# Windowed attention and a gated feed-forward on one core: regrouping the sums and products of an attention block, loading keys earlier, and halving the last projection

## Chip, cores, metric

One of the eight cores of a Trainium2 chip runs the whole kernel. The metric is device time in microseconds (us); lower is better. The profile's span is some 1.8 us shorter than the device time (335.7 and 337.54 for the profiled run of the kernel before). Executions of one kernel differ by some tenths of a us.

## The reference

Attention with a causal window of 64 positions over 8 batches, 8 heads, 576 positions and 64 values a head, then a gated feed-forward over the 4608 resulting rows of 512:

```python
scores = scale * np.matmul(q, k.transpose(0, 1, 3, 2))
mask = (rel >= 0) & (rel < 64)                  # rel = query position - key position
attn = softmax(np.where(mask, scores, -1e9))
x = np.matmul(attn, v)                          # (4608, 512) after the heads are joined
out = (silu(x @ w_gate) * (x @ w_val)) @ w_out  # 512 -> 1536 -> 512
```

## The kernel before

The rows are worked off in nine blocks `t` of 512. A block has an attention part, 12 pairs of gate matmuls (`gate_value`), and four projections (`project`). The projections of block `t - 1` run between the attention pieces of block `t`. One attention piece handles a pair `u` of heads:

- `scores`: 36 small matmuls on 64x64 tiles, an exponential on the scalar engine, and a mask product on the vector engine;
- `sums`: two matmuls with a weight of ones on 128x64 tiles, then a logarithm and the exponential of its negative on the scalar engine, which gives one over the sum;
- `values`: 16 matmuls on 128x64 tiles and a scaling on the vector engine.

The parts concerned (cuts marked by "..."):

```python
def values(t, u, o_ps):
    E = weights.pop((t, u))
    ...
    for m in range(8):
        for h in range(2):
            nc.tensor.matmul(blocks(o_ps[64 * h:64 * h + 64], t, m, m + 1), ..., blocks(E[:, h, :], t, m, m + 1))
    nc.vector.tensor_mul(xT[t][:, u, :], o_ps[:], inverse.pop((t, u)))

def products(t, u):
    sums(t, u, ...)
    values(t, u, ...)

# block 0's gates: block 1's keys are loaded at m = 3..6, cast at 7..10,
# transposed on the tensor engine at 8..11; queries are transposed from m = 10 on
...
# first phase: block 1's attention beside block 0's projections
for u in range(4):
    scores(1, u)
    if u % 2:
        project_part(0, (0, 1), halves, range(3 * u - 3, 3 * u + 3))
...
# every later phase
for u in range(8):
    if u < 4:
        scores(t, u)
    else:
        products(t, u - 4)
    if u % 2:
        project(t - 1, u // 2)
```

The softmax here doesn't subtract the row's maximum and nothing guards it: scores larger than these inputs give would overflow.

## Time and profile before

| | before |
|---|---|
| device time, median of the first 3 runs | 337.47 us |
| span of the profiled run | 335.7 us |
| tensor engine busy | 323.2 us, 96% |
| gate matmuls of block 1 begin at | 56.29 us |
| from one block's first gate to the next block's | 34.80 us |
| from the last block's first gate to the end of the span | 35.72 us |

The last three rows cut the run into start, seven equal periods and tail: 56.29 + 243.69 + 35.72. The starts are read from the tensor engine's timeline. A period is 20.7 us of gates and a phase of about 14 us of attention and projections. The first mark, as the timeline has it (start, length, what it was):

```profile
56.29 1.03 PE L306 MATMUL g_ps<-xT,wg 128*128 128x512 bf16 x4
```

One more row of the page of before, the busy share of the 16 DMA engines in 40 slices of 8.4 us (9 means 90% or more):

```profile
DMA  7999999999899499639931999199401320010013
```

After the first slice, the DMA engines are busy for 80% or more of the time until 100 us.

### The profile page before, as it was taken

The numbers are of one execution on the slowest core, as the hardware profiler recorded it, in microseconds if no ns is written. First come the engines' busy times: TensorE is split into PE (matmuls) and PEld (weight loads), VectorE is DVE, ScalarE is ACT, GpSimd is POOL, SyncE is SP. The second block draws the span as 40 slices with busy tenths as digits, with TensorE's granted clock in tenths as the row PEclk, the third lists the DMA queues.
The fourth block names the chain that finished last, engine by engine and source line by source line (L and its number), as shares of the span: only waits on it lengthen the run. The fifth ranks groups of instructions, "written<-read, shape, count | busy, mean of one in ns | idle before, by whom it ended". The sixth has DMA issues, their size and how long they took to land.

```text
span 335.7 us, 6932 instructions
## 1 busy us (share of the span) xinstructions
PE 323.2 (96%) x2683; PEld 153.9 (46%) x2729; DVE 214.2 (64%) x318; ACT 169.2 (50%) x241; POOL 137.8 (41%) x247
## 2 busy tenths in 40 slices
PE   8899799999999999999999999999999999999994
PEld 3444344444544454445444544444444444544441
DVE  5754766588667756785678656865786476753431
ACT  4764656336733763366435553565347633763300
POOL 5944345946767965256123896163200000000000
PEclk9999999999999999999999999999999999999999
DMA  7999999999899499639931999199401320010013
GB/s 261 205 202 226 229 188 223 125 205 215 147 248 186 52 176 234 124 58 209 185 89 20 170 180 167 12 189 177 111 0 48 79 56 3 23 72 31 3 32 94
DMA packets 83057, 44.12 MB, mean 131 GB/s; under 512 B 63824, under 2 KB 77648, under 8 KB 83024
## 3 DMA queue, kind: packets, MB, share of 16 engines
q0 software_dynamic: 49328, 22.56, 54.2%
q1 hardware_dynamic: 31680, 19.02, 20.6%
q10 hardware_dynamic: 2016, 2.10, 2.2%
q8 instruction: 21, 0.34, 0.4%
q14 instruction: 12, 0.10, 0.1%
HBM read 54.00 MB, written 9.44 MB: 189 GB/s over the span
## 4 chain that ended last, share of the span: by engine, by line
PE 88%; DMA 6%; DVE 3%; issue 2%; ACT 1%; DVEq 0%
PE g_ps L306 26%; PE v_ps L306 26%; PE o_ps L315 25%; PE s_ps L227 3%; DMA k_f<-in_k_dram 3%; PE ao_ps L271 3%; PE d_ps L245 3%; DMA q_f<-in_q_dram 1%; PE tp L174 1%; PE g_ps L286 1%; ACT E L233 1%; DVE kT L177 1%; PE v_ps L286 1%; DMA out_dram<-os__4409 1%; DMA out_dram<-os__4428 1%
## 5 line engine op out<-in xcount | busy, mean ns | idle before, releaser
L299 ACT ACTIVATE sg<-g_ps 128x512 f32<-128x512 f32 x108 | 64.4, 597 | 112.1 <-PE g_ps L306 79.9
L300 DVE TENSOR_TENSOR hT<-sg,v_ps 128x512 bf16<-128x512 f32 x108 | 74.9, 694 | 62.9 <-PE v_ps L306 59.9
L306 PE MATMUL v_ps<-xT,wv 128*128 128x512 bf16 x417 | 108.3, 379 | 0.5
L306 PE MATMUL g_ps<-xT,wg 128*128 128x512 bf16 x413 | 107.6, 379 | 0.5
L315 PE MATMUL o_ps<-wo,hT 128*128 128x512 bf16 x405 | 96.5, 380 | 1.6 <-issue 0.6
L107 POOL DMA_DIRECT2D k_s<-in_k_dram x112 | 60.7, 551 | 29.8 <-DMA q_s<-in_q_dram 20.5
L306 PEld LDWEIGHTS <-wv 128*128 128x128 bf16 x424 | 41.5, 98 | 50.0
L306 PEld LDWEIGHTS <-wg 128*128 128x128 bf16 x424 | 41.4, 98 | 49.5 <-issue 0.3
L315 PEld LDWEIGHTS <-hT 128*128 128x128 bf16 x432 | 39.6, 98 | 45.1 <-issue 0.4
L233 ACT ACTIVATE E<-s_ps 128x1024 bf16<-128x1024 f32 x36 | 35.2, 1021 | 8.4 <-PE s_ps L227 8.2
L277 DVE TENSOR_TENSOR xT<-ao_ps,r 128x512 bf16<-128x512 f32 x36 | 24.7, 691 | 22.7 <-ACT r L256 20.5
L196 DVE STREAM_TRANSPOSE kT<-k_s 128x512 bf16<-128x512 bf16 x28 | 35.9, 1284 | 0.0
L253 ACT ACTIVATE r<-d_ps 128x512 f32<-128x512 f32 (+1 forms) x35 | 21.0, 601 | 22.4 <-PE d_ps L245 22.4
L235 DVE TENSOR_TENSOR E<-E,mask 128x1024 bf16<-128x1024 bf16 x28 | 20.5, 739 | 11.5 <-ACT E L233 11.5
L87 POOL DMA_DIRECT2D q_s<-in_q_dram x28 | 15.3, 558 | 26.7 <-DVE qT L186 16.0
L148 POOL CAST v<-v_f 128x512 bf16<-128x512 f32 x22 | 14.3, 665 | 21.5 <-DMA v_f<-in_v_dram 17.5
L256 ACT ACTIVATE r<-r 128x512 f32<-128x512 f32 (+1 forms) x35 | 22.3, 641 | 1.1
L186 DVE STREAM_TRANSPOSE qT<-q_s 128x512 bf16<-128x512 bf16 x32 | 22.3, 702 | 0.0
L271 PEld LDWEIGHTS <-v 128*64 128x64 bf16 x576 | 13.8, 112 | 5.7 <-issue 1.7
L271 PE MATMUL ao_ps<-E,v 128*64 128x64 bf16 x576 | 15.3, 196 | 0.6 <-DVE v L156 0.6
L245 PE MATMUL d_ps<-E,ones 128*64 128x512 bf16 x72 | 13.9, 392 | 0.3
L227 PE MATMUL s_ps<-qT,kT 64*64 64x128 bf16 (+1 forms) x640 | 12.5, 211 | 0.2 <-DVE kT L177 0.2
(95 smaller groups left out, 175.6 us busy)
## 6 DMA issues: line engine op xcount, KB each, us to landing
q_s<-in_q_dram POOLq DMA_DIRECT2D x28, 248.0 KB, 6.7
k_s<-in_k_dram POOLq DMA_DIRECT2D x112, 56.0 KB, 5.2
v_f<-in_v_dram SPq DMA_DIRECT2D x22, 256.0 KB
v<-in_v_dram POOLq DMA_DIRECT2D x18, 128.0 KB, 4.8
k_f<-in_k_dram ACTq DMA_DIRECT2D x6, 256.0 KB
wo<-in_moe_w_out_dram POOLq DMA_DIRECT2D x3, 512.0 KB, 16.0
v<-v SPq DMA_DIRECT2D x6, 256.0 KB
v<-v SPq DMA_DIRECT2D x6, 192.0 KB
```

Of the source, the lines that this page charges most:

```text
L107: nc.gpsimd.dma_start(k_s[p0:p0 + 32, g, :, 0:w], k[b, a:H:2, s:s + P].rearrange("u (r e) d -> r u (e d)", e=4) [:, :, 32 * c:32 * c + w],)
L186: nc.vector.transpose(queries[t][:, u, :].rearrange("r (e x) -> r e x", e=16), staged[t][0][:, u].rearrange("r (e d) -> r e d", d=D)[:, :, ...
L196: nc.vector.transpose(dst[:, u, :].rearrange("r (g x e) -> r g e x", g=4, e=4), k_s[:, :, u].rearrange("r g (e d) -> r g e d", d=D)[:, :, ...
L227: nc.tensor.matmul(blocks(s_ps[64 * c:64 * c + 64, h], t, lo, hi), zero[r] if src is None else src[r, u, x:x + 64], blocks(qT[r], t, lo, h ...
L233: nc.scalar.activation(E[:], s_ps[:], AF.Exp, scale=0.125)
L245: nc.tensor.matmul(d_ps[64 * h:64 * h + 64], ones[:, 0:D], weights[t, u][:, h, :])
L271: nc.tensor.matmul(blocks(o_ps[64 * h:64 * h + 64], t, m, m + 1), (v1, v2)[m // 4][t % 2][:, m % 4, 2 * u + h, :] if t == LAST else (v2, v ...
L277: nc.vector.tensor_mul(xT[t][:, u, :], o_ps[:], inverse.pop((t, u)))
L299: nc.scalar.activation(sg[:], g_ps[:], AF.Silu)
L300: nc.vector.tensor_mul(hT[t][:, m, :], sg[:], v_ps[:])
L306: nc.tensor.matmul(ps[:], w[:, c, P * m:P * m + P], xT[t][:, c, :], start=(c == 0), stop=(c == 3),)
L315: nc.tensor.matmul(o_ps[:], hT[t][:, c, P * s:P * s + P], wo[:, c, :], start=(c == 0), stop=(c == 11),)
```

## The change

Its intent is to visit the small matmul tiles less often: in each phase the sums of pairs 0 and 1 follow the last scores, and the sums of pairs 2 and 3 and all four products form one group ahead of the last projection. With it come the edits of a sibling kernel (another version of the same program): keys of block 1 two gates earlier, another order at the start, a finer warm-up, and a last projection in two halves. The core of the diff, shortened and partly put in words:

```diff
-    def products(t, u):                      # sums and product of one pair
+    def finish_values(t):
+        for u in (2, 3):
+            sums(t, u, d_tile())
+        tiles = wide("ao_ps"), wide("ao_ps")
+        for u in range(4):
+            mix(t, u, tiles[u // 2][:, u % 2])      # the 16 matmuls
+        for u in range(4):
+            scale(t, u, tiles[u // 2][:, u % 2])    # the vector engine's product
...
+    def project_last(t, s):                  # two halves of 256 columns, own copies and stores
...
-    nc.vector.memset(ones[:], 1.0)
+    nc.vector.memset(ones[:, 0:P], 1.0)
+    nc.vector.memset(ones[:, P:512], 1.0)
-    keep_warm(7)
+    six warm-up matmuls of 128 columns, then keep_warm(6)
...
-    values(0, 0), values(0, 1), log_of(2), gates of m = 0, log_of(3), gates of m = 1
+    log_of(2), values(0, 0), values(0, 1), log_of(3), gates of m = 0 and 1
...
-        if 3 <= m < 7:      # key loads of block 1
+        if 1 <= m < 5:      # and casts, transposes two gates earlier, queries one
...
-            for u in range(8): (as above)
+            for u in range(4):
+                scores(t, u)
+                if u == 1:
+                    project(t - 1, 0)
+            for u in range(2):
+                sums(t, u, d_tile())
+            for s in (1, 2):
+                project(t - 1, s)
+            finish_values(t)
+            project(t - 1, 3)
...
-    for s in range(4):
+    for s in range(3):
         project(NT - 1, s)
+    project_last(NT - 1, 3)
```

The first phase gets the new grouping as well.

More of the change, by code (lines that the diff above doesn't have):

```diff
@@ L263, in sums, with mix @@
         inverse[t, u] = r
-    def values(t, u, o_ps):
+    def mix(t, u, o_ps):
         E = weights.pop((t, u))
-        if u == 0:
-            xT[t] = att.tile([P, 4, 512], BF16, name="xT", tag="xT")
         for m in range(8):
@@ L276, in values, with scale, wide, d_tile @@
                 )
-        nc.vector.tensor_mul(xT[t][:, u, :], o_ps[:], inverse.pop((t, u)))
-    def products(t, u):
-        sums(t, u, ps_f.tile([P, 512], FP32, name="d_ps", tag="v")[:])
-        values(t, u, ps_a.tile([P, 2, 512], FP32, name="ao_ps", tag="a")[:, 0])
+    def scale(t, u, o_ps):
+        if u == 0:
+            xT[t] = att.tile([P, 4, 512], BF16, name="xT", tag="xT")
+        nc.vector.tensor_mul(xT[t][:, u, :], o_ps, inverse.pop((t, u)))
+    def values(t, u, o_ps):
+        mix(t, u, o_ps)
+        scale(t, u, o_ps)
+    def wide(name):
+        return ps_a.tile([P, 2, 512], FP32, name=name, tag="a")
+    def d_tile():
+        return ps_f.tile([P, 512], FP32, name="d_ps", tag="v")[:]
+    def finish_values(t):
[6 more added lines that the diff above has]
+            scale(t, u, tiles[u // 2][:, u % 2])
     def gate_part(t, ms, tiles, c):
@@ L342, in project @@
         project_end(t, s, o_ps)
+    def project_last(t, s):
+        rows = out[S * batch(t):S * batch(t) + 512].rearrange("(r e) f -> e r f", e=16)
+        os_ = fsb.tile([P, 512], FP32, name="os_", tag="os_", bufs=3)
+        tiles = out_tile(), out_tile()
+        for x in range(2):
+            f = slice(256 * x, 256 * x + 256)
+            for c in range(12):
+                nc.tensor.matmul(
+                    tiles[x][:, 0:256], hT[t][:, c, P * s:P * s + P], wo[:, c, f],
+                    start=(c == 0), stop=(c == 11),
+                )
+            nc.vector.tensor_copy(os_[:, f], tiles[x][:, 0:256])
+            for i in range(4):
+                eng = nc.scalar if i % 2 else nc.sync
+                eng.dma_start(rows[4 * s + i][:, f], os_[32 * i:32 * i + 32, f])
     def set_exp():
@@ L368, in keep_warm @@
             nc.tensor.matmul(warm[0:D], ones[:, 0:D], ones[:])
-    keep_warm(7)
+    for _ in range(6):
+        nc.tensor.matmul(warm[0:D, 0:P], ones[:, 0:D], ones[:, 0:P])
+    keep_warm(6)
     nc.gpsimd.memset(tri[:], 1.0)
@@ L402, in shift_dma @@
         nc.sync.dma_start(dst, src)
-    def wide(name):
-        return ps_a.tile([P, 2, 512], FP32, name=name, tag="a")
     def join(copy, dst, src):
@@ L469, in log_of @@
         log(inverse[0, u], d_ps)
-    keep_warm(6)
+    keep_warm(5)
+    log_of(2)
     for u in range(2):
         values(0, u, ps_f.tile([P, 512], FP32, name="ao_ps", tag="gv"[u])[:])
-    log_of(2)
+    log_of(3)
     pairs = [gate_tiles() for _ in range(2)]
-    gate_part(0, (0,), pairs, 0)
-    log_of(3)
-    gate_part(0, (1,), pairs[1:], 0)
+    gate_part(0, (0, 1), pairs, 0)
     for u in (2, 3):
@@ L499 @@
             nc.vector.tensor_copy(mask[:, 1], mask[:, 0])
-        if 3 <= m < 7:
-            hs = slice(2 * m - 6, 2 * m - 4)
+        if 1 <= m < 5:
+            hs = slice(2 * m - 2, 2 * m)
             load_runs(nc.scalar, raw_k[:, hs], k, 1, hs)
-        if 7 <= m < 11:
-            u = m - 7
+        if 5 <= m < 9:
+            u = m - 5
             join(on_a, keys[:, u], raw_k[:, 2 * u:2 * u + 2])
-        if m >= 8:
-            u = m - 8
+        if 6 <= m < 10:
+            u = m - 6
             tp = ps_a.tile([P, 512], BF16, name="tp", tag="a")
@@ L510 @@
             split_k(kT[1][:, u, :], tp[:])
-        if m >= 10:
-            turn_q(1, m - 10)
-    turn_q(1, 2)
+        if m >= 9:
+            turn_q(1, m - 9)
     turn_q(1, 3)
@@ L527 @@
         shift_v(1, on_v, i, i + 1)
-    def d_tile():
-        return ps_f.tile([P, 512], FP32, name="d_ps", tag="v")[:]
     for u in range(2):
@@ L534 @@
     project(0, 2)
-    o_ps = out_tile()
-    for u in range(4):
-        if u < 2:
-            sums(1, u + 2, d_tile())
-        values(1, u, one("ao_ps"))
-        if u:
-            project_part(0, (3,), (o_ps,), range(4 * u - 4, 4 * u))
-    project_end(0, 3, o_ps)
+    finish_values(1)
+    project(0, 3)
     for t in range(1, NT):
@@ L546 @@
             set_exp()
-            for u in range(8):
-                if u < 4:
-                    scores(t, u)
-                else:
-                    products(t, u - 4)
-                if u % 2:
-                    project(t - 1, u // 2)
+            for u in range(4):
[8 more added lines that the diff above has]
+            project(t - 1, 3)
         set_silu()
```

## The prediction

> **What bounds the kernel now.** I read the page first (busy shares, then the chain that ended last), then the tensor engine's timeline piece by piece, then the timelines of the engines that issue loads.
>
> ```profile
> span 335.7 us, 6932 instructions
> PE 323.2 (96%) x2683; PEld 153.9 (46%) x2729; DVE 214.2 (64%) x318; ACT 169.2 (50%) x241; POOL 137.8 (41%) x247
> PE 88%; DMA 6%; DVE 3%; issue 2%; ACT 1%; DVEq 0%
> ```
>
> The tensor engine carries 88% of the chain. The clock row of the page is full in all 40 slices, so its matmuls cannot get cheaper; only the places where it waits or changes shape are to be had. In the timeline four 512-column matmuls start 0.86 us apart (160.69, 161.55, 162.41), 0.216 us each. The gate stage of 864 and the projection of 432 of them are 1296 x 0.216 = 280 us of the 335.7. The other 56 us are the start, eight attention phases and the tail.
>
> A steady phase is one attention block beside the four projections of the block before. Its two-pair stretch, from the tensor engine's timeline (start, length):
>
> ```profile
> 152.53 0.81 PE L315 MATMUL o_ps<-wo,hT 128*128 128x512 bf16 x3
> 153.27 0.41 PE L245 MATMUL d_ps<-E,ones 128*64 128x512 bf16 x2
> 153.51 0.42 PE L271 MATMUL ao_ps<-E,v 128*64 128x64 bf16 x16
> 153.76 0.39 PE L245 MATMUL d_ps<-E,ones 128*64 128x512 bf16 x2
> 153.98 0.42 PE L271 MATMUL ao_ps<-E,v 128*64 128x64 bf16 x16
> 154.33 0.82 PE L315 MATMUL o_ps<-wo,hT 128*128 128x512 bf16 x2
> ```
>
> No line shows an idle time: the engine never waits there for another. By starts the phase runs 146.70, 147.29, 149.99, 150.58, 153.27, 154.33, 157.03, 158.09, 160.69: scores 0.59, projection 2.70, scores 0.59, projection 2.69, two pairs 1.06, projection 2.70, two pairs 1.06, projection 2.60; 13.99 us. A projection of 12 x 0.216 is 2.59, so 0.10 of each 2.70 is the step to a smaller tile; the last, followed by gates of its own shape, lacks it.
>
> The one real wait is where the first phase begins (block 1 beside projections of block 0):
>
> ```profile
> 39.58 0.40 PE L174 MATMUL tp<-identb,k_b 128*128 128x128 bf16 x4
> 39.94 0.41 PE L227 MATMUL s_ps<-qT,kT 64*64 64x128 bf16 x16
> 42.02 0.22 PE L227 MATMUL s_ps<-qT,zero 64*64 64x64 bf16 x2 [1.66 <-DVE qT L186]
> 42.38 2.76 PE L315 MATMUL o_ps<-wo,hT 128*128 128x512 bf16 x11
> ```
>
> The second scores wait 1.66 us for a query transpose on the vector engine, which queued behind the last key copies; those waited for the late key load (the chain has a 9.63 us piece of that load from 29.26).
>
> **What the Trainium skill says.** "TensorEngine Tiling (Array Packing)", Key Properties: changing the tiling mode drains the engine. The trace agrees: 0.10 us in front of each smaller shape, and another 0.10 behind (ao products take 0.25 when products follow, 0.35 when a projection does). "DMA: Bandwidth & Descriptors", Queues, rings and completion order: each DMA engine goes round-robin between its queues. The page's DMA row is at nine tenths until some 100 us, and queue 0 alone took over a full share of the first 60 us, so an earlier key load displaces other loads and adds no bandwidth. "TensorE: Matmul & The Clock Gate", Part 1: the clock opens by a free-running window of about 3.4 us. The trace's warm-up matmuls are 0.427 apart from 1.53 us (cold) and 0.216 at 13 us; whether it opens earlier after the change no view can tell me.
>
> **The change part by part.**
>
> *Seven steady phases.* Before: four visits to small tiles. After: three, but the second goes scores, then sums (64x64 to 128x64), which is a mode change too. At the start scores take as long before 128x64 warm-up matmuls (12.39 to 12.73) as before 128x128 transposes (10.54 to 10.88), so that inner step costs what a way out costs. And two pairs of sums ahead of a projection leave late:
>
> ```profile
> 48.36 0.62 PE L245 MATMUL d_ps<-E,ones 128*64 128x512 bf16 x4
> 48.99 2.75 PE L315 MATMUL o_ps<-wo,hT 128*128 128x512 bf16 x12
> ```
>
> 0.63 for four sums, of which 2 x 0.216 is streaming. New phase: scores 0.59, projection 2.70, scores 0.59, sums 0.63, two projections 2.59 + 2.70, sums 0.24 + 0.22, products 3 x 0.25 + 0.35, projection 2.60: 13.96 against 13.99. So 7 x 0.03 = 0.2 us, almost nothing. New waits? The first sums need the masked weights of pair 0 and 1; masks of 0.69 start at 148.91 and 149.83, so are done at 150.52, while the sums would start at about 150.6: it just fits. The inversions and four scalings (0.69 each) end under the last projection.
>
> *First phase.* The four key loads go out two gates (3.45 us) earlier, the key transposes and the query transposes with them. The 1.66 wait goes, and scores take 0.59 in place of 2.44 (39.94 to 42.38). Two interleaved product visits also go. In block 0, the fourth sums no longer split the first gate matmuls:
>
> ```profile
> 16.38 0.38 PE L286 MATMUL v_ps<-xT,wv 128*128 128x512 bf16 x1
> 16.69 0.41 PE L245 MATMUL d_ps<-E,ones 128*64 128x512 bf16 x2
> 17.02 0.39 PE L286 MATMUL g_ps<-xT,wg 128*128 128x512 bf16 x1
> ```
>
> 16.16 to 17.56 becomes 4 x 0.216 + 0.10 = 0.96, a gain of 0.44. But the projections then meet their own weights. From the pool engine's timeline (brackets: what it waited for):
>
> ```profile
> 39.98 0.55 POOL L87 DMA_DIRECT2D q_s<-in_q_dram  x1 [2.15 <-DMA wo<-in_moe_w_out_dram]
> 42.55 0.54 POOL L87 DMA_DIRECT2D q_s<-in_q_dram  x1 [2.03 <-DMA wo<-in_moe_w_out_dram]
> ```
>
> The output weights come in thirds issued at 23.65, 26.53 and 27.84 and land 15.7 to 16.9 us later: at about 39.7, 42.3 and 44.8. Moving the key load inside a saturated stretch that ends after it leaves these times where they are. Without waits, projections would begin at about 39.6 and ask for the second third 8 matmuls later, at 41.3. It lands at 42.3, so I place that matmul at 42.37. Four matmuls (0.86), step and scores (0.10 + 0.59): 43.92. Four more: 44.78, where the last third has just landed (44.85); eight: 46.58. Step and sums 0.73: 47.31. Projection 2.59: 49.90. Step, sums, products 0.10 + 0.46 + 1.10: 51.56. Projection 2.59: 54.15. The gates began at 56.29, so 2.1 us are gained, including what the 0.44 can still give. The values of block 1 (last issue 35.06, median 13.8 us to landing) are there by about 48.9 and shifted by about 50.0, so products at 50.5 should not wait for them.
>
> *End.* The last projection goes in two halves of 256 columns. Today:
>
> ```profile
> 331.26 0.69 DVE L322 COPY os__4447<-o_ps 128x512 f32<-128x512 f32 x1 [1.90 <-DMA out_dram<-os__4428]
> 331.98 0.78 SPq L334 DMA_DIRECT2D out_dram<-os__4447  x2
> ```
>
> The skill ("Perfetto Trace Analysis", Optimizing Scalar/DVE Operations) gives the vector engine about 125 ns of overhead on PSUM. The trace has no 256-wide copy of this kind; as an estimate, (0.69 - 0.125)/2 + 0.125 = 0.41, so 0.28 less, minus 0.03 for 24 matmuls at 0.108 with one more start. The stores after it (some 3.7 us to the end of the span) keep most of their length at half the bytes. Gain 0.25.
>
> *Warm-up.* Memset and matmuls start perhaps 0.3 us earlier, but the transposes at 4.79 wait for the query load (3.27 us) and its cast (0.63): nothing, and an earlier clock would be swallowed by the weights at 42.3.
>
> Sum: 2.1 + 0.2 + 0.25 = 2.55; I keep 2.4, as a late key cast can delay gates by some tenths. 337.47 - 2.4 = 335.1.
>
> **Rivals.** (a) The small-tile visits cost more than starts show, and one fewer in seven phases gives 0.2 each: 1.4 us, about 333.9. Against it: the sums of projections, scores, sums and products above close to 0.03. (b) Sums right behind the last scores wait for the mask of pair 1, or four grouped products hold the score buffers and xT comes late: 0.3 x 7, about 337. Against it: the mask is done 0.1 before, and the scaling has 0.4 us and four gate matmuls to spare. (c) The earlier key load pushes gate weights or block 1's queries (issued 17.42 to 21.10, landing 13 to 15 us later, until 36.5) so late that the vector engine blocks: 1 us lost, 336.1. (d) The output weights land earlier or the wait is smaller: the first phase gains 3.2, about 334.
>
> **Range and chances.** (b) and (c) set the top, (a) and (d) the bottom: 333.7 to 336.4. Faster by 2% means below 330.7, which would need three times the sum: 2%. Slower by 2% needs a wait of over 1 us in each of seven phases: 1%.
>
> **What would show it.** Right: no 1.66 wait; an idle of about 1 us before an o_ps matmul at about 42.3 put down to output weights; gates of block 1 beginning near 54.2; steady phases of 13.9 to 14.0 us without idle; a last copy of about 0.4 us. Wrong: steady phases under 13.8 or over 14.2; idle before d_ps released by a mask; gates of block 0 delayed by weights.

## The result

334.94 us (median of 4 runs, 334.73 to 335.19) against 337.62 (4 runs, 337.40 to 338.62). The ratio is 0.9915, with a 95% interval of 0.9894 to 0.9936: 0.9% faster, which is clear of the noise. Ratios are the mean time of one kernel's fast runs over that of the other's of the same rounds, so they are not quite the ratio of the medians quoted. The fourth run of the kernel before, 338.62, has no clock on record; it may belong to the slow group described under late_keys. The forecast was 335.1, in a range of 333.7 to 336.4.

The page of the changed kernel:

```profile
span 333.1 us, 6959 instructions
PE 322.3 (97%) x2702; PEld 154.8 (46%) x2745; DVE 212.0 (64%) x320; ACT 168.3 (51%) x241; POOL 138.1 (41%) x247
PE 85%; DMA 12%; POOL 2%; issue 1%; DVE 0%; SPq 0%
```

Where 2.6 us went, cut by cut:

| | before | after | gain | forecast |
|---|---|---|---|---|
| until the gates of block 1 | 56.29 | 54.88 | 1.41 | 2.1 |
| seven periods | 243.69 | 243.18 | 0.51 | 0.2 |
| from the last block's first gate to the end | 35.72 | 35.01 | 0.71 | 0.25 |

The DMA share of the chain doubled, from 6% to 12%. The chain of waits in the first 60 us, read back from block 1, shows why (start, length, what it was):

```profile
15.94 14.97 DMA wg<-in_moe_w_gate_dram
30.91 0.28 issue
31.20 14.34 DMA wo<-in_moe_w_out_dram
45.54 0.04 issue
45.58 0.38 PE o_ps L332
```

The last gate weights land at 30.91. Only after that does the pool engine issue the last third of the output weights, which lands at 45.54. What the tensor engine did before that point no longer counts for block 1. In seven traces with this first phase (the two of the changed kernel, one_tail, late_warm, old_phases, old_start and late_keys_fill) this third lands between 45.06 and 45.57, and in each of them the gates of block 1 begin 9.34 or 9.35 us later. The tensor engine's timeline in the first phase (in brackets: idle time before, and what ended it):

```profile
39.92 0.22 PE L227 MATMUL s_ps<-qT,zero 64*64 64x64 bf16 x2 [0.70 <-DVE qT L186]
40.28 1.90 PE L332 MATMUL o_ps<-wo,hT 128*128 128x512 bf16 x7
42.58 1.02 PE L332 MATMUL o_ps<-wo,hT 128*128 128x512 bf16 x4 [0.40 <-DMA wo<-in_moe_w_out_dram]
44.12 1.04 PE L332 MATMUL o_ps<-wo,hT 128*128 128x512 bf16 x4
45.58 1.89 PE L332 MATMUL o_ps<-wo,hT 128*128 128x512 bf16 x7 [0.42 <-DMA wo<-in_moe_w_out_dram]
54.88 1.03 PE L323 MATMUL g_ps<-xT,wg 128*128 128x512 bf16 x4
```

The forecast wait is there, as two waits for two weight thirds, and a query wait of 0.70 is left of the 1.66. A steady phase, from its second scores to the next gates (it begins at 145.30; some projection matmuls are missing from the record):

```profile
148.88 0.37 PE L227 MATMUL s_ps<-qT,kT 64*64 64x128 bf16 x14
149.18 0.62 PE L245 MATMUL d_ps<-E,ones 128*64 128x512 bf16 x4
149.73 5.35 PE L332 MATMUL o_ps<-wo,hT 128*128 128x512 bf16 x23
155.01 0.62 PE L245 MATMUL d_ps<-E,ones 128*64 128x512 bf16 x4
155.47 1.18 PE L269 MATMUL ao_ps<-E,v 128*64 128x64 bf16 x64
156.58 1.25 PE L332 MATMUL o_ps<-wo,hT 128*128 128x512 bf16 x4
159.18 1.03 PE L323 MATMUL g_ps<-xT,wg 128*128 128x512 bf16 x4
```

It takes 13.88 us, where 13.96 was forecast and 13.99 was the value before. One phase in this trace, block 3's, takes 14.10; the runs below say why. The last copy is half as wide:

```profile
329.37 0.42 DVE L372 COPY os__4423<-o_ps 128x256 f32<-128x256 f32 x1 [0.89 <-PE o_ps L368]
```

### The profile page after: what moved, and what is told of

Read it like the earlier page. It is cut to its first block, busy times and chain, and to the rows that moved or that the text cites. A ratio compares the mean times of both kernels' runs of the same rounds, so it can differ in the third digit from the quotient of the medians.

```text
span 333.1 us, 6959 instructions
## 1 busy us (share of the span) xinstructions
PE 322.3 (97%) x2702; PEld 154.8 (46%) x2745; DVE 212.0 (64%) x320; ACT 168.3 (51%) x241; POOL 138.1 (41%) x247
## 4 chain that ended last, share of the span: by engine, by line
PE 85%; DMA 12%; POOL 2%; issue 1%; DVE 0%; SPq 0%
PE o_ps L332 27%; PE g_ps L323 25%; PE v_ps L323 24%; DMA wg<-in_moe_w_gate_dram 4%; DMA wo<-in_moe_w_out_dram 4%; PE d_ps L245 3%; PE s_ps L227 3%; PE ao_ps L269 2%; DMA v_f<-in_v_dram 2%; DMA k_f<-in_k_dram 1%; PE o_ps L368 1%; POOL wv L160 1%; POOL wg L160 1%; POOL v L148 0%; DVE os__4423 L372 0%
## 5 line engine op out<-in xcount | busy, mean ns | idle before, releaser
L323 PE MATMUL v_ps<-xT,wv 128*128 128x512 bf16 x414 | 107.1, 379 | 0.2
L332 PE MATMUL o_ps<-wo,hT 128*128 128x512 bf16 x396 | 93.9, 380 | 2.3 <-DMA wo<-in_moe_w_out_dram 0.8
L279 DVE TENSOR_TENSOR xT<-ao_ps,r 128x512 bf16<-128x512 f32 x36 | 22.5, 683 | 6.1 <-PE ao_ps L269 6.1
L87 POOL DMA_DIRECT2D q_s<-in_q_dram x28 | 15.2, 552 | 26.2 <-DVE qT L186 15.6
L148 POOL CAST v<-v_f 128x512 bf16<-128x512 f32 x22 | 14.5, 676 | 18.5 <-DMA v_f<-in_v_dram 15.6
L94 POOL DMA_DIRECT2D q_s<-in_q_dram x16 | 8.6, 625 | 9.5 <-DVE qT L186 9.5
L269 PEld LDWEIGHTS <-v 128*64 128x64 bf16 x576 | 10.9, 112 | 3.3 <-issue 0.8
```

The costliest lines, as they stand in the source:

```text
L279: nc.vector.tensor_mul(xT[t][:, u, :], o_ps, inverse.pop((t, u)))
L323: nc.tensor.matmul(ps[:], w[:, c, P * m:P * m + P], xT[t][:, c, :], start=(c == 0), stop=(c == 3),)
L332: nc.tensor.matmul(o_ps[:], hT[t][:, c, P * s:P * s + P], wo[:, c, :], start=(c == 0), stop=(c == 11),)
```

## The experiments

Twelve kernels ran in three sets. The first and third set share a chip and its runs of the kernel before; the second has its own. All results were right, except where a wrong one is announced. "The changed kernel" on the first chip is run after_again. The first set (one_tail, late_warm, late_keys, old_phases) started from four guesses about where the 2.6 us came from, the second (keys_only, fill_wait, no_wo, thirds) from what the first showed, and the third is the rest. A run is said to have fallen when its clock was halved for a while.

**after_again: the changed kernel once more.** No edit.

> The changed kernel once more, unchanged, as the yardstick for the other three on the same chip: 334.7 to 335.3, clock 0.997 or more in every run, block 3's phase with gates between 34.69 and 35.3.

334.59 us (6 runs, 334.30 to 334.81), clock 0.998 to 1.0; ratio 0.9886 (0.986 to 0.9912). Four of the six lie under the stated range, which began at 334.7. Gates of block 1 begin at 54.63. The larger gain than in the first comparison comes from the kernel before, which fell into its slow group in 6 of 12 runs here. That is explained under late_keys.

**one_tail: the last projection in one piece.**

```diff
-    for s in range(3):
+    for s in range(4):
         project(NT - 1, s)
-    project_last(NT - 1, 3)
```

> The changed kernel with its last projection in one piece of 512 columns again. Theory from comparing the two traces: the two halves are worth about 0.7 us (last copy 0.69 against 0.42, last store's landing 2.39 against 2.17 us after its issue, closing waits 1.34 against 1.11 us), so the time goes up by 0.6 to 0.8 and everything ahead of the last projection stays. Rival, my prediction's own figure: only the shorter copy counts, +0.25.

335.18 us, 0.59 over after_again. From the last block's first gate to the end it takes 35.7 us, as before the change, against 35.0. The copy:

```profile
328.91 0.69 DVE L339 COPY os__4436<-o_ps 128x512 f32<-128x512 f32 x1 [1.90 <-DMA out_dram<-os__4417]
```

It ends at 329.60, 3.8 us before the end of a span of 333.4. With halves it ends at 329.79, 3.3 us before the end of 333.1. So 0.27 us come from the copy and 0.5 from what follows it. In the trace the sync engine's closing wait for the last store ends 2.39 us after that store's issue in one_tail and 2.17 in the changed kernel, and the rest takes 1.34 against 1.07 us (1.11 in the expectation is a misreading). In that rest seven short waits of 0.06 us each follow in one_tail and three in the changed kernel, where the others are over by then. The theory stands; the forecast's 0.25 counted the copy alone.

**late_warm: the old warm-up.**

```diff
-    nc.vector.memset(ones[:, 0:P], 1.0); nc.vector.memset(ones[:, P:512], 1.0)
-    (six warm-up matmuls of 128 columns); keep_warm(6)
+    nc.vector.memset(ones[:], 1.0)
+    keep_warm(7)
```

> The changed kernel with the old warm-up (one memset of 512 columns, seven wide warm-up matmuls). Theory: the clock opens at about 6.9 us instead of 4.6, the first eight transposes stand 0.107 apart again and block 0's gates start some 0.6 us later, but the first phase still waits for the output weights at about 45.5 us, so gates of block 1 begin within 0.2 us of 54.9 and the time is the same (within 0.2). Rival: the earlier clock is worth its lead, and the time goes up by 0.6.

334.46 us, 0.13 under after_again, and block 1's gates begin at 54.67: the time is the same. But the reasoning was wrong in part. The clock opened at 5.1 us with the old warm-up, and block 0's gates began at 20.17, no later than in after_again (20.35). Over all traces it opens between 3.8 and 7.4 us with either kind (old: 6.9, 4.3, 7.4, 5.1; new: 3.8 to 7.1), so no effect of the finer warm-up on it can be seen. By chance this trace holds the clearest view of a small loss. Block 3's phase took 14.5 us, because the mask of pair 1 was late for the sums. The vector engine, and below it the pool engine at the same time:

```profile
113.31 1.51 DVE L235 TENSOR_TENSOR E<-E,mask 128x1024 bf16<-128x1024 bf16 x1 [0.22 <-ACT E L233]
```
```profile
113.07 2.35 POOL L593 COPY maskl<-tri 128x64 bf16<-128x64 bf16 x8
```

The mask product takes 0.69 us in other blocks, and 1.51 while the pool engine copies. The sums of pair 1 come 0.6 us later. The overlap alone does not decide it, though. In old_start the same copies run beside the same mask product, and there the copies are slow (3.29 us for eight, against 1.89 at 110.53 in the changed kernel, beside no mask) and the mask is not:

```profile
113.51 0.71 DVE L235 TENSOR_TENSOR E<-E,mask 128x1024 bf16<-128x1024 bf16 x1 [0.22 <-ACT E L233]
112.74 3.29 POOL L597 COPY maskl<-tri 128x64 bf16<-128x64 bf16 x8
```

In the first trace of the changed kernel it is the pool engine's casts of the values, from 113.03 on, that run beside the slow masks. Which of the two engines gives way was not tested. This is rival (b) of the forecast, in one phase of seven and not in every execution (34.69 to 35.30 for block 3's period).

**late_keys: keys and queries of block 1 as late as before.** The offsets of the key loads, casts, key transposes and query transposes are those of the kernel before.

```diff
-        if 1 <= m < 5:       # loads; casts from 5, key transposes from 6, queries from 9
+        if 3 <= m < 7:       # loads; casts from 7, key transposes from 8, queries from 10
```

> The changed kernel with block 1's key loads, casts, transposes and query transposes where they were before. Theory: the wait for a query transpose ahead of the second scores comes back (1 to 2 us), gates of block 1 begin at about 56 and the time goes up by 1.0 to 1.5. Rival: the output weights pin the phase anyway, so the move is worth under 0.4.

Neither the theory nor the rival fits all runs. They fall into two groups: 334.45, 334.92 and 335.11 at a mean clock of 0.999 to 1.0, and 336.25, 336.35 and 336.41 at 0.995. The first group equals the changed kernel, so in these runs the earlier keys were worth nothing or little (medians 334.92 and 334.59). The record counts both groups as fast. The profiled run is of the second group:

```profile
40.93 0.22 PE L227 MATMUL s_ps<-qT,zero 64*64 64x64 bf16 x2 [1.69 <-DVE qT L186]
40.94 0.41 PE L227 MATMUL s_ps<-qT,kT 64*64 64x128 bf16 x16
41.28 4.45 PE L332 MATMUL o_ps<-wo,hT 128*128 128x512 bf16 x12
```

Twelve matmuls that take 2.76 us elsewhere take 4.45, without a wait. The engines' busy times by stretch (start:end, length, busy of PE, PEld, DVE, ACT, POOL, then the granted clock, DMA share and GB/s) say why:

```profile
41.00:42.00 1.00, 1.00 (x20) 0.47 (x21) 1.00 (x3) 0.86 (x2) 0.00 (x0) 0.67 1.24 211
43.00:44.00 1.00, 1.00 (x4) 0.39 (x3) 0.23 (x1) 0.00 (x0) 0.15 (x1) 0.50 1.95 168
45.00:46.00 1.00, 1.00 (x30) 0.46 (x32) 0.00 (x0) 0.00 (x0) 0.54 (x1) 1.00 2.30 146
```

The clock is halved from 41.35 us for 3.41 us, which costs 3.41 / 2 = 1.7. The wait of 1.69 us just ahead of it is the suspect. The kernel before has the same wait and the same two groups: on this chip six runs at 337.14 to 337.77 with a clock of 0.996 to 1.0, and six at 338.95 to 339.43 with 0.993 or 0.994.

Why only some executions fall can be worked out from the traces. In both traces that fell (this one and keys_only) the clock falls a whole number of times 3.413 us after it opened: 11 times here (3.80 to 41.35), 4 times there (4.28 to 17.93). Count windows of this length from the opening in all 14 traces, up to 325 us, and add up the tensor engine's idle time in each, by its timeline. The two falls come at the end of the two windows with the most, 1.71 and 1.46 us; every other window has at most 1.10 us, and none of those is followed by a fall. In the trace of the kernel before, which did not fall, such a mark at 41.07 cuts the wait in two (it lasts from 40.36 to 42.02). So whether a wait of 1.7 us costs anything seems to depend on where it lies between the marks; no run set out to test this.

**old_phases: blocks 2 to 8 in the old order.**

```diff
-            (scores, projection, scores, sums 0-1, two projections, finish_values, projection)
+            for u in range(8):
+                if u < 4: scores(t, u)
+                else: sums(t, u - 4, ...); values(t, u - 4, ...)
+                if u % 2: project(t - 1, u // 2)
```

> The changed kernel with blocks 2 to 8 in the old order (sums and product of each pair together, two visits). Theory from the traces: each phase takes 13.99 instead of 13.88, so +0.6 to +0.8 over seven, less 0.2 for the one mask wait that goes: +0.5. Rival, my prediction's working: 13.99 against 13.96, +0.2. Second rival: the grouping costs something elsewhere, and the time falls.

335.17 us, 0.58 over after_again. Seven periods take 243.69 us, just as in the kernel before, against 242.97 (after_again) and 243.18 (first trace). So the grouping is worth 0.10 us a phase, 0.72 in all, less what block 3's mask takes back.

**keys_only: the kernel before with nothing but the earlier keys.**

```diff
-        if 3 <= m < 7:       # and the casts and transposes that follow
+        if 1 <= m < 5:
```

> The kernel before with nothing changed but the earlier key loads, casts and transposes. Theory: the long wait ahead of the second scores shrinks from 1.7 to about 0.7 us and the projections of block 0 then wait for the output weights; gates of block 1 begin about 0.9 us earlier (55.4), the time is about 336.3, and no run has its clock fall for a window, so all runs lie within 0.8 of each other at a mean clock of 0.996 or more. Rival: the two-peaked times of the kernel before (337.2 at a clock of 0.996 to 1.0, 339.1 at 0.993 to 0.994) have nothing to do with this wait, and both peaks stay, 1.8 apart.

336.32 us (336.01 to 336.80); the kernel before in this set 337.53 (11 runs: nine at 337.27 to 337.78, two at 338.77 and 339.12 with a clock of 0.993). Against those nine, whose median is 337.47, that is 1.15 us. Its profiled run had its clock halved as well, at 17.9 us, after a wait of 1.07 us for gate weights and others around it; its clock of 0.995 is that of the run of 336.80. The first phase began late there, waited for nothing, and the gates of block 1 began at 55.57 all the same. So this edit alone gains about 1.1 us, and none of its six runs lies at 339; that no run's clock falls was wrong.

**fill_wait: the kernel before with its wait filled.**

```diff
         scores(1, u)
+        if u == 0:
+            fill = ps_f.tile([P, 512], FP32, name="fill", tag="v")
+            for _ in range(7):
+                nc.tensor.matmul(fill[0:D], ones[:, 0:D], ones[:])
```

> The kernel before with seven warm-up matmuls into a spare tile between the first and the second scores of block 1, where it waits 1.7 us. They fill the wait and take nothing away. Theory: the wait lets the clock fall by half for one window of 3.4 us in about half of the runs, which costs 1.7; filled, all runs stay at a clock of 0.996 or more and at 337.0 to 337.9. Rival: the second peak comes from late loads, stays in about half of the runs at 339, and the fill costs up to 0.3 more.

337.50 us, all six runs at 337.33 to 337.71 with a clock of 0.997 to 0.999: no slow group. The fill lies where the wait was and moves nothing:

```profile
40.22 1.70 PE L523 MATMUL fill<-ones 128*64 128x512 bf16 x7
41.98 0.22 PE L227 MATMUL s_ps<-qT,zero 64*64 64x64 bf16 x2
```

**late_keys_fill: late_keys with the same seven matmuls.** The edit is late_keys and fill_wait together.

> The changed kernel with the late keys (run late_keys, where three of six runs lay at 336.3 with a clock of 0.995) and seven warm-up matmuls in the wait ahead of the second scores. Theory: the earlier keys gain nothing but the clock: no run falls to 0.995, and all six lie within 0.4 of the changed kernel. Rival: the wait itself costs, and all runs lie 1.0 to 1.5 above the changed kernel.

334.70 us (334.38 to 334.98), clock 0.998 to 1.0: the slow group is gone, and the time is within 0.11 of after_again (334.59). The two fills together: none of 12 runs fell, where 11 of 29 of the same kernels without a fill did (8 of 23 of the kernel before, 3 of 6 of late_keys). The wait causes the slow group. (fill_wait alone would not show it: in its set only two of 11 runs without the fill fell.) And with the rest of the change in place the earlier keys gain nothing but the clock, because the output weights come no sooner.

**no_wo: two thirds of the output weights not loaded.**

```diff
-    weights_o(4, 8)
-    weights_o(8, 12)
+    nc.gpsimd.memset(wo[:, 4:12, :], 0.0)
```

> The changed kernel with the last two thirds of the output weights set to zero by the pool engine in place of loads (so the result is wrong on purpose). Theory: the first phase is held up by the landing of those two thirds only (0.40 + 0.42 us in the trace of the changed kernel), so gates of block 1 begin at about 54.0 and the time falls by 0.8. Rival: another late arrival (block 1's queries or values) takes their place and the time falls by under 0.3.

Wrong result, as announced; 334.14 us (333.36 to 334.70). The projections run through from 40.32 without a wait, and block 1's gates begin at 53.78, 0.85 to 1.1 before those of the two traces of the changed kernel (54.63 and 54.88). The projections began at 40.28 with the weights too, so the whole lead arises where the two waits were. The landing of the output weights is what held the first phase up. The total scatters too much for a figure.

**thirds: the projections cut where the weights arrive.**

```diff
-            project_part(0, (0, 1), halves, range(3 * u - 3, 3 * u + 3))
+            project_part(0, (0, 1), halves, range(2 * u - 2, 2 * u + 2))
...
+    (sums of pairs 0 and 1)
+    project_part(0, (0, 1), halves, range(8, 12))
+    (loads of block 2 moved up, ahead of the sums)
+    (copies, sums of pairs 2 and 3, third projection, products, fourth projection)
```

> The changed kernel with block 0's first two projections cut at the borders of the three weight loads: columns 0 to 3 after the first scores, 4 to 7 after the second, then the sums of pairs 0 and 1, and only then 8 to 11; the sums of pairs 2 and 3 cover the copy of the results. Theory: the waits for the output weights are filled with work that has to be done anyway, gates of block 1 begin at about 54.4 in place of 54.9, and the time falls by 0.4. Rival: the extra visit to small tiles and the shift of the values on the vector engine eat it, within 0.2.

334.01 us (5 runs, 333.96 to 334.18), ratio 0.9889 (0.9871 to 0.9908). Gates of block 1 begin at 54.35; of the two weight waits one of 0.32 us is left. This is the lowest time of a correct kernel here, but the changed kernel did not run in its set. Against the unfallen runs of before of each set thirds is 337.47 - 334.01 = 3.46 below, after_again 337.42 - 334.59 = 2.83. By the traces 0.3 of this difference lies in the first phase and 0.1 at the end. I take it as 0.3 to 0.6 us, not as settled.

**old_start: the old order at the start of block 0.**

```diff
-    keep_warm(5); log_of(2); values(0, 0-1); log_of(3); gate_part(0, (0, 1), pairs, 0)
+    keep_warm(6); values(0, 0-1); log_of(2); gate_part(m = 0); log_of(3); gate_part(m = 1)
```

> The changed kernel with the old order of logarithms and gate matmuls at the start of block 0. Theory: block 0's gates start 0.4 later, but the output weights pin the first phase, so gates of block 1 stay within 0.2 of 54.9 and the time within 0.3. Rival: the 0.44 us come back in full.

334.49 us, 0.10 under after_again. Block 0's gates begin at 21.41, 1.1 later than in after_again (20.35; 0.4 was expected; the clock opened at about the same time, 5.6 and 5.4 us), and block 1's at 54.88 against 54.63. The last third of the output weights landed at 45.54 against 45.29, the same 0.25 later. A head start at the front is swallowed by the weights.

**best: thirds with a mask built earlier and the last projection cut at 384.** It was meant to beat the rest.

```diff
-        for x in range(2):                       # 256 + 256 columns
+        for x, (lo, hi) in enumerate(((0, 384), (384, 512))):
...
-            k_l = load_k(...); (maskl copies)
+            (maskl copies); k_l = load_k(...)
```

> Run thirds with two more edits: the mask for the last block is built ahead of the second key load rather than after it (so that the pool engine's casts no longer run beside block 3's masks), and the last projection is cut at 384 columns instead of 256. Expected: gates of block 1 at 54.4 (as in thirds), block 3 at 34.69 and no more, the last copy 0.29 instead of 0.42, 0.8 to 1.0 under the changed kernel on the same chip. If the casts still run beside the masks, block 3 stays at up to 35.3; if four stores of 512 bytes a row land no sooner, the last gain is nil.

335.00 us, 0.41 over after_again: a miss in three places. The third projection waited for the copy of the first result:

```profile
48.19 2.75 PE L332 MATMUL o_ps<-wo,hT 128*128 128x512 bf16 x12 [0.57 <-DVE os__800 L339]
```

Block 3 took 34.91, as the pool engine's casts from 113.86 on still ran beside a mask. And from the last block's first gate to the end it took 35.4 us against 35.0: with 384 columns the first stores are issued at 329.00 (328.52 with 256), and the last ones only at 329.88, 0.5 us after the last copy is done. Why thirds did not meet the wait for the copy, this one trace of each does not settle.

## Why the prediction was right

The total was right: 2.4 us forecast, 2.6 measured in the spans, 2.7 in the medians. The mechanism of the largest term was right too; its size, and those of two smaller terms, were not. That the total fits so well is luck: the first phase gained 0.7 us less than forecast, the phases 0.3 and the end 0.45 more.

- **"Seven steady phases", 13.96 against 13.99.** Measured 13.88. Scores into sums (0.59), two projections (5.28 against 5.29), sums (0.46) and products (1.11 against 1.10) came out as worked. The mis-sized term is "sums 0.63", the four sums ahead of a projection: 0.555 when they follow scores. The 0.63 was read where they follow a projection, and still holds there (0.635 at 47.40). What decides the 0.08 was not tried.
- **Rival (b), the mask that "just fits".** It fits in six phases. In block 3's, in some executions, it is 0.2 to 0.6 us late, where copies or casts of the pool engine run beside it and it takes up to 1.51 in place of 0.69. I had looked at mask durations in one phase only.
- **First phase, 56.29 to 54.15.** Measured 54.88, and 54.4 to 54.9 in the seven traces named above. From the landing of the last third on the working was right: 9.30 us (44.85 to 54.15), measured 9.34. So 0.69 of the 0.73 us that were missing are this landing, at 45.54 in place of 44.85; the mis-sized step is "Moving the key load inside a saturated stretch ... leaves these times where they are". The second third landed at 42.5 where 42.3 was forecast. Why the last one came later is open. Its issue moved from 27.84 to 31.20, but in late_keys_fill it was issued at 29.50 and landed no earlier (45.57); and the 44.77 of the one trace at hand is the earliest of all: fill_wait, with the loads of the kernel before, has 45.19. The queries landed at 37.8 in place of 36.5, rival (c) in a mild form: this left the wait of 0.70, which the weights swallow. no_wo confirms that these weights hold the phase.
- **Block 0, the 0.44 "can still give".** In the changed kernel's first trace it gave nothing: the stretch from the first gate matmul to the products of pair 2 took 1.40 us, as before (15.42 to 16.82; 16.16 to 17.56), because the second gate matmul came 0.65 us after the first in place of 0.22, with an idle time of 0.28 put down to its weights. The prediction had named "gates of block 0 delayed by weights" as a sign of being wrong, and "idle before d_ps released by a mask" as another. Both came true in small, the second with 0.41 us in late_warm.
- **What the step gave too much credit.** It began from the 1.66 us wait. late_keys_fill shows that, with the rest of the change in place, removing that wait is worth 0.1: the reordered start and the grouping already bring the engine to the weights in time. The parts replace one another: keys alone gain 1.1, and all without keys gain as much as all with them.
- **End, 0.25.** Measured 0.7. The copy was estimated at 0.41 and took 0.42; "The stores after it ... keep most of their length" was the mis-sized step: of some 3.7 us after the copy 0.5 went.
- **Warm-up, nothing.** Right.
- **What the prediction did not see:** the kernel before loses 1.7 us in 8 of 23 runs because its wait lets the clock fall. The first three times of before held no such run, and I took the wait for a cost of its own length. With it the average gain is larger than forecast (ratio 0.9886 where half of the runs of before fell).

## What to carry to other kernels

When loads are saturated at the start, find the landing that ends the last wait there. Here every gain ahead of it was swallowed, and edits did not add up: the keys alone gained 1.1, and all the rest without them as much as all together. A wait can cost more than its length when the clock falls after it (1.69 us of waiting cost another 1.7 here); two groups of times with two mean clocks are the sign, and idle matmuls in the wait are a cheap test. Cut the span at fixed marks and compare piece by piece: here the steady phases were off by 0.08 us each and the tail by 0.45, and the first phase by 0.7 the other way, which the total hid.

## What the Trainium skill lacked or had wrong

- "TensorE: Matmul & The Clock Gate", "Why this matters for your kernels", asks for no idle gaps over about 3 us between bursts, or one window of idle brings the clock back to half. Here half a window of idle time or less was followed by half clock: windows of 3.41 us with 1.71 us of it (late_keys, nearly all of it one gap of 1.69) and with 1.46 (keys_only, a wait of 1.07 among others), and none with 1.10 or less. The half clock lasted 3.41 us both times, which agrees with the page's window.
- The same page, Part 1, says that the opening varies by half a us either way with the phase of a free-running window. Here it opened between 3.8 and 7.4 us for matmuls that began at 1.1 to 1.5 us, with two kinds of warm-up. Counted from the first matmul that is 2.7 to 5.9 us, a spread of nearly a whole window; a warning further down in the same part (6 to 14 slow matmuls for one kernel) fits this better.
- "TensorEngine Tiling (Array Packing)", Key Properties, says that a mode change drains the engine but gives no cost. Here it is about 0.10 us on the way in and 0.10 on the way out of a group of small matmuls; scores into sums, a change between two small modes, took 0.117 us from the last start to the next.
- "SBUF — State Buffer", Who interferes with whom, says that a vector instruction with two SBUF inputs contends with pool instructions that read SBUF. The traces agree and give the size here: a mask product of 0.69 us took 1.51 beside copies of the pool engine (late_warm), or the copies took 3.29 in place of 1.89 and the mask product 0.71 (old_start).
- No page says that the end of a kernel depends on how the last store is cut: 256 columns in place of 512 saved 0.5 us after the copy, and a cut at 384 lost 0.4 against 256.
